# Another order of issue for a fused attention and two-layer-MLP kernel, and a changed rule for sending queued products

## The chip, the cores and the metric

The kernel runs on one core of a Trainium2 chip. The time is the device time of one execution in microseconds (us), the median of several runs. The engines are called by the names that the profile uses: PE (matrix products; PEld its weight loads), DVE, ACT and POOL (the three engines that work element by element), and SP (which issues the transfers). PSUM is the accumulator memory in eight banks, which PE writes and which ACT and DVE read; SBUF is the working memory.

## The reference

A local attention over 7 tokens feeds two MLPs one after the other; all is float32. There are 8192 tokens of 192 values, and both MLPs have a hidden width of 2048.

```python
w = softmax(weight_gen)                       # per token, 8 heads x 7 taps
x1[s] = sum over k of w[s, :, k] * x[s + k - 6]   # 24 values to a head
h = x1 @ moe_w_in;  g = h * sigmoid(h);  x2 = g @ moe_w_out
h = x2 @ moe2_w_in
P = a0 + a1*h + a2*h*h + a3*h*h*h
Q = 1 + abs(b0)*abs(h) + abs(b1)*h*h
out = (P / (Q + 1e-6)) @ moe2_w_out
```

## The kernel before

**Tiling.** The tokens go in 16 batches `b` of 512. In each batch either MLP's hidden width is cut into 8 units `u` of 256, so a unit is a tile of 128 partitions by 1024 values (two PSUM banks, tile `h`). Products are made in two parts (a rounded high part and the rest, the tiles that end in `h` and `l`), so that one matrix product of float32 is several products of PE. PE works as two halves of 64 rows, called lanes; the instructions of a product are dealt to both lanes.

**The operations by letter.** An operation is named letter, unit, batch, as `u3.15`.

| letters | engine | what |
|---|---|---|
| A, K and B, Q | PE | first products of MLP 1 and of MLP 2 into the bank `h`, in two halves |
| S, H, L | ACT, ACT, DVE | MLP 1: silu in place in `h`, its high part `g1h`, its low part `g1l` |
| C, E, I, F and D, P, J, R | PE | second products of MLP 1 and MLP 2 into `acc0`, `acc1` |
| U (line 921), V (line 925) | ACT | MLP 2: `t = a3*h + a2`; `y = abs(b1*h)`. Both read the bank `h` |
| u (line 931), w (line 934) | DVE | `t = t*h`; `t = (t + a1)*h`. Both read the bank `h`; w is the last reader |
| Y, N, G, g | DVE, ACT, ACT, DVE | the denominator, its log, the exponential of minus that, the quotient; all from SBUF |
| h, l | POOL, ACT or DVE; DVE or POOL | high and low part of the quotient (`g2h`, `g2l`) |
| M, m, p, r, a | POOL or DVE | the attention of one token column: two products, three additions |
| T, XH, XL; EC, EM, EA; FC, FT, FE, FA, O | all | turning and splitting the input; handing MLP 1 to MLP 2; turning and storing the output |

**The order of work.** All 3957 operations stand in one written list, `ORDER`. An entry gives the operation, the engine where it may choose (`@1` is the second in its list), and the buffer or bank slot after a colon; `^` loads ACT's tables first and `|` shifts the clocks of PE's lanes. `Plan.run` goes through the list from first to last; each engine gets its own operations in that order and then works through them strictly in turn, waiting at semaphores for what an operation needs. A product entry is not written out at once: `Lanes.add` queues its instructions by lane, and `Lanes.take` writes them as both lanes have something. When an operation of another engine needs a product that is still queued, `Lanes.drain` writes out the queue up to it, even if only one lane has anything:

```python
lanes.drain(past if engine == "PE" else past | need)
```

`Lanes.take` also puts an empty step on SP (line 372) where a bank changes from one pairing of lanes to the other; PE waits for that step.

Of the kernel before, what the change touches and what calls it, by code (L numbers as in the profile page):

```python
# [39 lines left out]
    s0l X.0 q0B0l0:e s1l q0B0l1:d Z.0 q0A0l1:m q0A0l0:q q0O1l1:r q0O0l0:j q0O1l0:g q0O0l1:h q0A1l0:x cl s2l:p  # L40
    q0A1l1:k s0m s0d ^^s0e s0t s0n M0.0@1:v M1.0@1:i cn cz:f q0B0a0 s1m q0B040:B q0B0a1 q0B041 M2.0:b q0A0a0 q0B0h1
    q0A0a1 m2.0@1:l M3.0@1:d m0.0@1:t m1.0@1:y p0.0 p1.0 p2.0 m3.0@1:c r0.0 p3.0 r2.0 a0.0@1:u r3.0@1 r1.0@1 a3.0
    a2.0 a1.0 s1d@1 q0A040:C q0B0h0 q0O0a0 q0B0x1 q0A041 q0O040:D q0B0x0 q0A0h q0O0a1 q0O041 q0A0x W0.0:A T.0 TR.0
    W1.0:B XH0.0:w XL0.0:y A0.0 q0O1a0 ca q0O0h s1e q0O1a1 q0O140:C q0A1a0 X.1 q0O3l0:v s1t q0O141 q0O0x s2m q0O1h@1
    q0O1x cr A1.0:A K0.0 K1.0 A2.0:D K2.0 ^S0.0 S1.0 H0.0:c H1.0:e q1B0l0:i q0O2l0:q q0O3l1:u q0O2l1:h q1O1l0:a
    q1O0l1:s L0.0:t L1.0:j I0.0:C s2d@1 q0A1a1 S2.0 ^^s2e q0A140:A q0A141 q0A1h@1 q0A1x |I1.0 F0.0 A3.0:B C1.0 K3.0
    E0.0 E1.0 C0.0 s2t ^S3.0 H3.0:x q0O2a0 H2.0:c q0O2a1 L3.0:t A5.0:A L2.0:d q0O240:D q0O241 s1n@1 M3.1:m m2.1:g
    M2.1:o m3.1:b p2.1@1 p3.1@1 s2n@1 m1.1:l r2.1@1 M1.1:q p1.1@1 M0.1:l m0.1:h p0.1@1 r0.1@1 r3.1@1 r1.1@1 a0.1:h
    a1.1 a2.1 a3.1 F1.0 K5.0 S5.0 H5.0:k q1B0l1:g s2s q1A0l0:r q1A0l1:b A4.0:B F3.0 F2.0 K4.0 I2.0 L5.0:n q0O3a0
    q0O2h S4.0 q0O3a1 q0O2x H4.0:j q0O340:D q0O341 L4.0:u q1B0a0 q1B0a1 q0O3h@1 q1B040:B q1B041 q0O3x |A6.0:A I3.0  # L50
    K6.0 C5.0 C4.0 C3.0 E5.0 E3.0 E2.0 S6.0 H6.0:p q1A0a0 q1B0h1 q1A0a1 q1B0h0 L6.0:x q1O0l0:v q1O1l1:e X.2 AW.2
    q1A1l0:i q1A1l1:g |||A7.0:D I4.0 K7.0 E4.0 C2.0 E6.0 C6.0 S7.0 H7.0:d q1B0x1 q1A040:A q1B0x0 q1A041 L7.0:o
    ||C7.0 T.1:B ||E7.0 TR.1 F7.0 F6.0 F4.0 I7.0 I6.0 F5.0 I5.0 q1O0a0 q1A0h q1O040:D q1O0a1 q1A0x q1O1a0 XH0.1:q
    q1O041 q1O140:A q1O1a1 q1O0h XL0.1:y q1O141 q1O2l1:r q1O2l0:p q1A1a0 q1O0x q1O1h q1A1a1 EC.0:o q1A140:B q1A141
    q1O1x q1A1h q1A1x ||||||A2.1:D K2.1 EM.0 s3l:d m2.2:t M0.2:w m0.2:v p0.2@1 M1.2:b M2.2:j M3.2:x m3.2@1:u m1.2:e
    p3.2@1 r0.2@1 a0.2:n p1.2@1 r1.2@1 p2.2@1 A1.1:A K1.1 A3.1:B S2.1 H2.1:s L2.1:g q1O2a1 S1.1 q1O2a0 EA.0 s3m
    XH1.0:h A0.1:D K0.1 H1.1:v XL1.0:i K3.1 S0.1 H0.1:u L1.1:a q1O240:A S3.1 H3.1:m q1O3l0:c AW.3 X.3 q1O3l1:o
    L0.1:k B0.0:C Q0.0 q1O241 B5.0:D Q5.0 q1O2h V0.0:l U0.0:t L3.1:p q1O2x Y0.0 F3.1:B I3.1 B3.0:A V5.0:r U5.0:w
    u0.0 w0.0 u5.0 w5.0 r2.2@1 a1.2 r3.2@1 a2.2 s3d@1 a3.2 m0.3:x E3.1 C2.1 Q3.0 F1.1 F2.1 I1.1 B2.0:C C3.1 E2.1
# [218 lines left out]
class Plan:  # L278
# [24 lines left out]

    def run(self, engines, preload, lanes):


        done, final, uses, held = set(), {}, {}, {}
        for entry in ORDER.split():
            name = entry.strip("^|").partition(":")[0].partition("@")[0]
# [4 lines left out]
        for entry in ORDER.split():  # L314
# [3 lines left out]
            if table:  # L318
                preload(table)
# [778 lines left out]
```

## Time and profile before

| | |
|---|---|
| median of 3 runs | 1350.39 us (1350.03 to 1350.97) |
| the profiled execution, its own time | 1347.33 us |
| its span, first to last instruction | 1345.5 us |
| busy: PE, DVE, ACT, POOL | 91%, 83%, 78%, 41% of the span |
| chain that ended last: PE, DVE, ACT, issue | 37%, 28%, 20%, 7% |

The profile is of one execution. Its time is 3.06 us under the median of the runs, and 1.8 us of it lie outside the span. The chain that ended last is followed back from the last instruction, at each step to what released it or to the instruction before it on its engine. A wait names the engine and line whose instruction came last of those waited for.

### The profile page before, as it was taken

The page shows a single profiled execution, that of the slowest core. Times are in us where ns is not written, and L with a number is a line of the kernel's source. Part 1 is how long each engine was busy: PE and PEld are TensorE (multiplying, and loading weights), DVE is VectorE, ACT ScalarE, POOL GpSimd, SP SyncE. Part 2 cuts the span into 40 slices and gives each one's busy share as a digit, 9 for nine tenths or more (in the row PEclk, how much of TensorE's full clock was granted, in tenths as well). Part 3 has the DMA queues.
Part 4 walks back from the last instruction along what each step waited for, and adds up shares of the span by engine and source line. Part 5 has one row for each costly group of instructions (what it writes and reads, how often), then busy time and mean ns, then how long its engine had stood idle before and what let it go on. Part 6 is the DMA issues. An engine that isn't in the chain of part 4 may idle for free.

```text
span 1345.5 us, 24941 instructions
## 1 busy us (share of the span) xinstructions
PE 1219.7 (91%) x10340; PEld 1038.0 (77%) x10340; DVE 1119.9 (83%) x1010; ACT 1047.9 (78%) x1018; POOL 545.7 (41%) x353
## 2 busy tenths in 40 slices
PE   5999998889989999989998898899989999899987
PEld 5668788778867788877786686787768778788866
DVE  7998998887979898887797776967868878887997
ACT  4888897877877886877887776877768778687885
POOL 3973463635454225346236333435312433330142
PEclk9989999999999999999999999999989999999999
DMA  8630011001020100100101010100000101000000
GB/s 224 217 102 1 23 49 41 1 1 50 1 67 1 38 34 1 53 1 20 48 1 50 14 54 1 25 32 2 20 0 2 53 1 50 1 20 1 10 1 36
DMA packets 17752, 45.41 MB, mean 34 GB/s; under 512 B 2412, under 2 KB 9194, under 8 KB 17640
## 3 DMA queue, kind: packets, MB, share of 16 engines
q1 hardware_dynamic: 17640, 43.83, 10.8%
q8 instruction: 81, 1.33, 0.4%
q14 instruction: 31, 0.25, 0.1%
HBM read 31.73 MB, written 7.90 MB: 29 GB/s over the span
## 4 chain that ended last, share of the span: by engine, by line
PE 37%; DVE 28%; ACT 20%; issue 7%; POOL 1%; SPq 0%; POOLq 0%; DVEq 0%; ACTq 0%
PE h L769 19%; PE acc L769 17%; DVE t L931 6%; DVE t L934 5%; ACT y L925 5%; DVE t L951 4%; DVE y L940 4%; ACT t L921 4%; ACT y L945 3%; ACT y L948 2%; DVE g1l L884 2%; DVE g2l L961 2%; ACT g1h L880 2%; ACT h L876 1%; ACT L1061 1%
## 5 line engine op out<-in xcount | busy, mean ns | idle before, releaser
L769 PE MATMUL h<-xh,wa 64*128 64x512 f32 x2048 | 475.0, 401 | 70.2 <-DVE t L934 39.0
L769 PEld LDWEIGHTS h<-xh,wa 64*128 64x128 f32 x2048 | 287.9, 186 | 132.4 <-issue 17.8
L769 PE MATMUL h<-xl,wa 64*128 64x512 f32 x1024 | 317.4, 392 | 0.1
L769 PE MATMUL h<-xh,wb 64*128 64x512 f32 x1024 | 316.4, 391 | 0.0
L769 PE MATMUL acc<-g1h,wo 64*128 64x512 f32 x1536 | 306.8, 397 | 8.1 <-ACT g1h L880 3.6
L769 PE MATMUL acc<-g2h,wo 64*128 64x512 f32 x1536 | 302.4, 397 | 10.0 <-DVE t L934 4.7
L961 POOL TENSOR_TENSOR g2l<-t,g2h 128x1024 fp32r<-128x1024 f32 x65 | 166.9, 2572 | 226.5 <-DVE g2l L961 72.0
L769 PEld LDWEIGHTS acc<-g2h,wo 64*128 64x128 f32 x1536 | 211.6, 186 | 37.8 <-SPq L372 7.9
L931 DVE TENSOR_TENSOR t<-t,h 128x1024 f32<-128x1024 f32 x128 | 155.4, 1215 | 101.0 <-ACT y L925 84.1
L769 PEld LDWEIGHTS acc<-g1h,wo 64*128 64x128 f32 x1536 | 214.5, 187 | 29.0 <-ACT g1h L880 6.3
L769 PE MATMUL acc<-g1l,wo 64*128 64x512 f32 x1024 | 219.1, 401 | 7.4 <-DVE g1l L884 5.8
L711 POOL TENSOR_TENSOR pr<-xw,aw 128x768 f32<-128x768 f32 (+1 forms) x90 | 149.9, 1678 | 181.8 <-PE acc L769 107.2
L769 PE MATMUL acc<-g2l,wo 64*128 64x512 f32 x1024 | 218.5, 396 | 3.8 <-ACT t L921 1.5
L884 DVE TENSOR_TENSOR g1l<-h,g1h 128x1024 fp32r<-128x1024 f32 x128 | 155.0, 1217 | 53.4 <-ACT g1h L880 47.8
L921 ACT ACTIVATE t<-h,a_sb 128x1024 f32<-128x1024 f32 x128 | 153.5, 1201 | 47.4 <-PE h L769 35.0
L925 ACT ACTIVATE y<-h,b_sb 128x1024 f32<-128x1024 f32 x128 | 141.5, 1110 | 60.8 <-DVE t L934 32.5
L940 DVE SCALAR_TENSOR_TENSOR y<-y,b_sb 128x1024 f32<-128x1024 f32 x128 | 179.7, 1410 | 6.2 <-ACT y L925 6.2
L876 ACT ACTIVATE h<-h 128x1024 f32<-128x1024 f32 x128 | 129.3, 1012 | 71.2 <-PE h L769 62.5
L951 DVE SCALAR_TENSOR_TENSOR t<-t,a_sb,y 128x1024 f32<-128x1024 f32 x128 | 181.7, 1431 | 3.5 <-ACT y L948 3.2
L945 ACT ACTIVATE y<-y,c_sb 128x1024 f32<-128x1024 f32 x128 | 145.7, 1148 | 43.1 <-DVE y L940 42.4
L436 POOL TENSOR_SCALAR g2h<-t 128x1024 fp32r<-128x1024 f32 x56 | 72.3, 1294 | 253.3 <-DVE t L951 182.6
L769 PEld LDWEIGHTS h<-xl,wa 64*128 64x128 f32 x1024 | 163.6, 186 | 12.8 <-DVE xl L803 1.0
(79 smaller groups left out, 1985.5 us busy)
## 6 DMA issues: line engine op xcount, KB each, us to landing
xw<-in_x_dram SPq DMA_DIRECT2D x14, 960.0 KB, 5.5
raw<-in_moe_w_out_dram SPq DMA_DIRECT2D x16, 383.5 KB, 6.4
out_dram<-of SPq DMA_DIRECT2D x15, 384.0 KB, 3.0
e<-e SPq DMA_DIRECT2D x32, 128.0 KB, 2.3
raw<-in_moe_w_in_dram SPq DMA_DIRECT2D x16, 255.9 KB, 6.7
raw<-in_moe_w_in_dram SPq DMA_DIRECT2D x4, 511.8 KB, 6.7
aw<-wsm SPq DMA_DIRECT2D x14, 112.0 KB, 2.8
sm<-in_weight_gen_dram SPq DMA_DIRECT2D x3, 448.0 KB, 3.8
```

What stands on the lines that cost most here:

```text
L436: pool.tensor_scalar(out=out, in0=in_, scalar1=1.0, scalar2=0.0, op0=ALU.mult, op1=ALU.add)
L711: e.tensor_tensor(out=p.rearrange("p k (h g) -> p k h g", g=G), in0=st[xw][:, j + k0:j + k0 + n, :].rearrange("p k (h g) -> p k h g", g=G) ...
L769: return pe.matmul(out=out, lhsT=w, rhs=x, start=start, stop=stop)
L876: act.activation(out=st[hb], in_=st[hb], func=AF.Silu)
L884: dve.tensor_tensor(out=t, in0=st[hb], in1=st[gh].bitcast(F32), op=ALU.subtract)
L921: act.activation(out=q, in_=st[hb], func=AF.Identity, scale=a_sb[:, 3:4], bias=a_sb[:, 2:3])
L925: act.activation(out=q, in_=st[hb], func=AF.Abs, scale=b_sb[:, 1:2])
L931: dve.tensor_tensor(out=st[t], in0=st[t], in1=flat(), op=ALU.mult)
L940: dve.scalar_tensor_tensor(out=st[y], in0=st[y], scalar=b_sb[:, 0:1], in1=st[y], op0=ALU.add, op1=ALU.mult)
L945: act.activation(out=st[y], in_=st[y], func=AF.Ln, scale=c_sb[:, 0:1], bias=1.0 + 1e-6)
L951: dve.scalar_tensor_tensor(out=st[t], in0=st[t], scalar=a_sb[:, 0:1], in1=st[y], op0=ALU.add, op1=ALU.mult)
L961: e.tensor_tensor(out=q, in0=st[t], in1=st[gh].bitcast(F32), op=ALU.subtract)
```

## The change

Two things change. First, `ORDER` is another list of the same 3957 operations. Second, `Plan.run` no longer writes out queued products when an operation of another engine needs them: it puts that operation, and all of other engines behind it, into a list `later`, and sends them once the products that they need have been written. A product that needs an operation in `later` sends that list up to it first. The lane clock also counts differently where one lane is empty. The table loads marked by `^` go with their operation.

```diff
+        later = []
+
+        def send():
+            _, after, engine, table, fn = later.pop(0)
+            lanes.drain(after)
+            if table:
+                preload(table)
+            fn(engines[engine])
+
...
-            if table:
-                preload(table)
...
             engine = names[int(e or 0)]
-            lanes.drain(past if engine == "PE" else past | need)
-            if engine == "PE" and name[0] != "W":
-                lanes.add(name, fn(engines[engine]), bars)
+            if engine != "PE":
+                later.append((name, past | need, engine, table, fn))
             else:
-                if engine == "PE":
+                while any(x[0] in need or x[0] in past for x in later):
+                    send()
+                lanes.drain(past)
+                if name[0] == "W":
                     lanes.drain()
-                fn(engines[engine])
+                    fn(engines[engine])
+                else:
+                    lanes.add(name, fn(engines[engine]), bars)
+            while later and not lanes.waiting(later[0][1]):
+                send()
+        while later:
+            send()
         lanes.drain()
...
-        self.clock[r] = max(self.clock[r], self.clock[1 - r] - 1) + turns if not self.queue[1 - r] else self.clock[r] + turns
+        self.now = max(self.now, self.clock[r])
+        self.clock[r] = self.now + turns
+
+    def waiting(self, names):
+        return any(self.left.get(n) for n in names)
...
-        while any(self.left.get(n) for n in (self.left if names is None else names)):
+        while self.waiting(self.left if names is None else names):
             r = int(self.clock[1] < self.clock[0])
-            if not self.queue[r]:
-                self.clock[r] = self.clock[1 - r]
-                r = 1 - r
-            self.take(r)
+            self.take(r if self.queue[r] else 1 - r)
```

All lines of `ORDER` change. A stretch of batch 15 of MLP 2 before and after:

```diff
-    Y0.15 V3.15:s g2.15 Y3.15 g1.15 U3.15:w N0.15 h2.15@1:o G0.15 U6.15:m V6.15:f g0.15 u6.15 Y6.15 B5.15:D P7.14
-    P5.14 P6.14 Q5.15 D4.14 u3.15 w6.15 N3.15 h0.15@1:q N6.15 G3.15 l2.15@1:u h1.15:l w3.15 V5.15:n |D2.15:A P2.15
...
+    B5.15:D P4.14 P7.14 D7.14 D4.14 D5.14 Q5.15 N1.15 V3.15:k G1.15 N0.15 U6.15:l V6.15:y Y3.15 g1.15 l2.15@1:c
+    u6.15 w6.15 G0.15 h1.15@1:s N3.15 g0.15 U3.15:w h0.15@1:v U5.15:g V5.15:t G3.15 Y6.15 N6.15 G6.15 l1.15@1:f
+    u3.15 w3.15 Y5.15 g3.15 l0.15:a g6.15 R2.15:A J2.15 J1.15 J4.14 D1.15 P2.15 D0.15 |B4.15:C P1.15 D2.15 Q4.15
```

Its beginning and its end before and after:

```diff
-    s0l X.0 q0B0l0:e s1l q0B0l1:d Z.0 q0A0l1:m q0A0l0:q q0O1l1:r q0O0l0:j q0O1l0:g q0O0l1:h q0A1l0:x cl s2l:p
...
+    s0l X.0 s1l q0B0l0:u q0B0l1:w Z.0 q0A0l0:g q0A0l1:i s2l:o q0O0l0:h q0O1l1:t q0O0l1:m q0O1l0:v cl q0A1l0:r s0m cn
...
-    D4.14 N7.14 G7.14 FE.14 u7.14 w7.14 g7.14 h7.14@2:b FA.14 l7.14:l ||D7.15 ||J7.15 R7.15 ||P7.15 FC.15:u FT.15:D
-    O.14 O.13 FR.15 FE0.15 FE1.15@1 FA0.15 FA1.15 O0.15 O1.15
...
+    u7.15 w7.15 g7.15 h7.15@2:x l7.15:c ||||P4.15 J4.15 R4.15 |J7.15 FT.14:C ||R7.15 FR.14 D7.15 P7.15 FC.15:f
+    ||FT.15:D FE.14@1 FA.14 O.13 O.14 FR.15 FE0.15 FE1.15 FA0.15 FA1.15 O0.15 O1.15
```

Counted over both texts of `ORDER`:

| | before | after |
|---|---|---|
| M on DVE, of 64 | 18 | 22 |
| m on DVE, of 64 | 20 | 25 |
| p on DVE, of 64 | 24 | 25 |
| r on DVE, of 64 | 20 | 27 |
| a on DVE, of 64 | 26 | 32 |
| h on POOL, ACT, DVE | 56, 50, 22 | 51, 45, 32 |
| l on DVE, POOL | 63, 65 | 62, 66 |
| EC on ACT, DVE | 13, 3 | 11, 5 |
| FC on ACT, DVE | 6, 10 | 11, 5 |
| FE on ACT, DVE | 7, 10 | 9, 8 |
| M, m, p, r, a, h, l on DVE between A0.3 and A0.5 | 23 | 34 |
| loads of ACT's tables | 91 | 85 |
| units in the order V U u w | 36 | 58 |
| units in the order U V u w | 65 | 39 |
| units in the order U u V w | 7 | 10 |
| units in the order U u w V | 20 | 21 |
| entries from U to u, median | 6 | 9 |
| entries from V to u, median | 4 | 7 |

## Rows read from the trace of the kernel before

**Rows 1.** The page, part 1: busy time, share of the span, instructions.

```profile
PE 1219.7 (91%) x10340; PEld 1038.0 (77%) x10340; DVE 1119.9 (83%) x1010; ACT 1047.9 (78%) x1018; POOL 545.7 (41%) x353
```

**Rows 2.** Windows by stage: stretch, length, busy of PE, PEld, DVE, ACT, POOL, clock, DMA.

```profile
29.00:120.00 91.00, 82.86 (x623) 63.32 (x623) 83.19 (x92) 73.86 (x83) 59.55 (x48) 0.94 0.41 130
120.00:760.00 640.00, 588.37 (x5085) 503.81 (x5084) 546.50 (x474) 508.24 (x484) 290.14 (x183) 1.00 0.08 26
760.00:1326.00 566.00, 521.21 (x4418) 447.98 (x4416) 458.76 (x402) 445.61 (x426) 180.62 (x105) 0.98 0.06 16
1326.00:1345.50 19.50, 12.81 (x110) 8.98 (x108) 10.13 (x12) 7.59 (x8) 2.41 (x1) 0.93 0.16 61
```

**Rows 3.** The page, part 4: the chain that ended last, by engine.

```profile
PE 37%; DVE 28%; ACT 20%; issue 7%; POOL 1%; SPq 0%; POOLq 0%; DVEq 0%; ACTq 0%
```

**Rows 4.** Groups by form: busy, mean ns | idle before them, and who ended it.

```profile
L921 ACT ACTIVATE t<-h,a_sb 128x1024 f32<-128x1024 f32 x128 | 153.5, 1201 | 47.4 <-PE h L769 35.0 <-DVE t L951 3.8 <-DVE g2l L961 3.8
L925 ACT ACTIVATE y<-h,b_sb 128x1024 f32<-128x1024 f32 x128 | 141.5, 1110 | 60.8 <-DVE t L934 32.5 <-DVE t L931 11.0 <-PE h L769 10.5
L931 DVE TENSOR_TENSOR t<-t,h 128x1024 f32<-128x1024 f32 x128 | 155.4, 1215 | 101.0 <-ACT y L925 84.1 <-ACT t L921 14.1 <-PE acc L769 2.6
L934 DVE SCALAR_TENSOR_TENSOR t<-t,a_sb,h 128x1024 f32<-128x1024 f32 x128 | 163.5, 1278 | 4.7 <-ACT y L925 1.2
```

**Rows 5.** The chain in order of time, three places: start us, us, what.

```profile
102.48 0.97 ACT y L925
...
103.54 0.06 DVE t L931
...
888.61 1.21 ACT t L921
889.81 1.01 ACT y L925
...
890.90 1.23 DVE t L931
...
892.16 1.29 DVE t L934
...
893.59 1.45 PE h L769 x10
...
1268.33 1.01 ACT y L925
...
1269.37 1.23 DVE t L931
```

**Rows 6.** All waits, two of them: us in total, times, longest us.

```profile
PE h L769 <- DVE t L934: 39.0, 28, 3.8
...
PEld h L769 <- SPq L372: 16.3, 39, 1.9
```

**Rows 7.** Groups by form, the operations that change their engine (columns of Rows 4).

```profile
L711 DVE TENSOR_TENSOR pr<-xw,aw 128x768 f32<-128x768 f32 x18 | 18.4, 1026 | 2.9 <-PE acc L769 1.6 <-DMA xw<-in_x_dram 1.3
L711 DVE TENSOR_TENSOR pr<-xw,aw 128x576 f32<-128x576 f32 x20 | 17.1, 866 | 0.8 <-PE acc L769 0.8
L725 DVE TENSOR_TENSOR pr<-pr 128x384 f32<-128x384 f32 x20 | 14.3, 716 | 0.2 <-POOL pr L721 0.2
L731 DVE TENSOR_TENSOR ao<-pr 128x192 f32<-128x192 f32 x26 | 11.3, 437 | 0.0
L438 DVE CAST g2h<-t 128x1024 fp32r<-128x1024 f32 x22 | 21.2, 969 | 0.2
L438 DVE COPY of<-acc 128x1024 f32<-128x1024 f32 x10 | 12.2, 1218 | 3.4 <-PE acc L769 3.4
L434 ACT ACTIVATE g2h<-t 128x1024 fp32r<-128x1024 f32 x50 | 52.4, 1053 | 8.4 <-DVE t L951 8.3
L434 ACT ACTIVATE of<-acc 128x1024 f32<-128x1024 f32 x6 | 6.1, 1022 | 4.8 <-PE acc L769 4.7
L1061 ACT ACT_TABLE_LOAD x46 | 59.0, 1283 | 1.5 <-PEq L1082 0.7
```

More of the change, by code (lines that the diff above doesn't have):

```diff
@@ L45 @@
[L45 to L59, printed above, removed]
@@ new lines @@
+    N7.10 FE.9 A1.12:C m3.13:r p3.13 FA.9 l2.10:e EM.11 A2.12:D K1.12 D3.10 O.9 X.14 EA.11 G6.10 G5.10 g5.10
+    XH1.11:g h4.10:v XL1.11:r K2.12 J4.10 A0.12:A P2.10 D4.10 ^S1.12 S2.12 H1.12:n g6.10 l3.10:k K0.12 R3.10
+    h6.10@1:a H2.12:c S0.12 H0.12:p r3.13 L1.12:x B2.11:C P3.10 Q2.11 l4.10@1:f L2.12:i r2.13@1 a2.13 a3.13 L0.12:v
+    U2.11:t V2.11:q B3.11:D R4.10 Q3.11 B0.11:A U3.11:h V3.11:l u2.11 w2.11 h5.10:w l6.10@1:k l5.10@1:j D6.10 Q0.11
+    u3.11 w3.11 Y2.11 Y3.11 ^^G7.10 U0.11:b V0.11:s N3.11 N2.11 G3.11 J5.10 J6.10 C2.12:C E2.12 R6.10 R5.10 E1.12
@@ new lines @@
+    L7.13:c H6.13:a I5.13 I7.13 F7.13 B7.12:A V4.12:w U4.12:f Y5.12 L6.13:d ^^N5.12 G5.12 u4.12 Y4.12 w4.12 g5.12
+    C6.13 E6.13 Q7.12 B6.12:B E7.13 C4.13 J0.12:D E4.13 C7.13 Q6.12 F6.13 J3.12 R0.12 R2.12 F4.13 R3.12 N1.12
+    U7.12:c G1.12 u7.12 V7.12:o E5.13 g1.12 h1.12:k w7.12 U6.12:r N4.12 G4.12 V6.12:t l1.12:h Y7.12 P3.12 T.14:A
+    D2.12 I6.13 F5.13 R1.12 TR.14 I4.13 D1.12 P0.12 P2.12 D3.12 D0.12 Y6.12 u6.12 w6.12 N7.12 XH0.14:e EC.13:l G7.12
+    N6.12 h5.12@2:n XL0.14:y EM.13 AW.15 X.15 O.11 A1.14:B g7.12 A0.14:A G6.12 K1.14 J5.12 J2.12 EA.13 g4.12
@@ new lines @@
+    XH1.13:j XL1.13:o h4.12@2:x l5.12:a ^S1.14 H1.14:l A2.14:C D4.12 L1.14:w K2.14 J4.12 B2.13:B R5.12 Q2.13
+    h7.12@1:u S2.14 H2.14:v U2.13:q l7.12:d M1.15@1:b g6.12 h6.12@1:i L2.14:g l6.12@1:m P1.12 P5.12 K0.14 J1.12
+    B0.13:C D5.12 Q0.13 D6.12 u2.13 w2.13 S0.14 H0.14:s V2.13:k L0.14:t A3.14:B V0.13:r U0.13:h J6.12 K3.14 S3.14
+    Y2.13 ^^N2.13 H3.14:i Y0.13 m1.15@1:c l4.12:n u0.13 w0.13 M0.15:a m0.15:p p0.15@1 D7.12 B1.13:A J7.12 R4.12
+    R6.12 Q1.13 L3.14:f p1.15 V1.13:u Y1.13 r0.15@1 U1.13:p G2.13 N1.13 G1.13 N0.13 u1.13 g2.13 w1.13 g1.13
@@ new lines @@
+    m3.15@1:c C1.14:C E2.14 E0.14 C2.14 R7.12 E1.14 B4.13:B P6.12 P4.12 I1.14 Q4.13 F3.14 P7.12 F0.14 F2.14 B3.13:A
+    I2.14 Q3.13 G0.13 U4.13:k FC.12:l a0.15@1:n u4.13 V4.13:x g0.13 E3.14 B5.13:D V3.13:t U3.13:d w4.13 M3.15@1:g
+    m2.15@1:a u3.13 r1.15@1 a1.15@1 w3.13 A4.14:B I3.14 Q5.13 C3.14 K4.14 ^S4.14 H4.14:f h2.13:v l2.13:i Y4.13
+    A7.14:A C0.14 L4.14:r p3.15@1 M2.15:m r3.15@1 K7.14 I4.14 F1.14 A5.14:B C4.14 U5.13:u S7.14 h0.13@1:w u5.13
+    w5.13 K5.14 I0.14 V5.13:b H7.14:c S5.14 H5.14:f A6.14:D E4.14 p2.15 Y3.13 a3.15 r2.15 L7.14:a K6.14 F4.14
@@ new lines @@
+    L5.14:g l0.13:e Y5.13 a2.15@1 h1.13:r l1.13@1:q S6.14 H6.14:s B7.13:A C7.14 FT.12:B E7.14 L6.14:m Q7.13 F7.14
+    FR.12 I7.14 FE.12@1 FA.12 ^^N3.13 G3.13 V7.13:a N4.13 U7.13:p I5.14 F6.14 B6.13:D D1.13:B P2.13 Q6.13 E5.14
+    C6.14 R2.13 J1.13 N5.13 Y7.13 G5.13 G4.13 u7.13 w7.13 g3.13 h3.13@2:i g5.13 g4.13 T.15:A R0.13 I6.14 TR.15 P0.13
+    F5.14 D2.13 D3.13 U6.13:o V6.13:r XH0.15:b E6.14 C5.14 Y6.13 XL0.15:g J2.13 J3.13 R1.13 A0.15:A J0.13 u6.13
+    h4.13@2:t h5.13:y EC.14:f O.12 EM.14 N6.13 G6.13 w6.13 g6.13 K0.15 D4.13 D5.13 A1.15:D N7.13 G7.13 EA.14
@@ new lines @@
+    XH1.14:c l5.13:e XL1.14:n l3.13@1:x J4.13 K1.15 D0.13 B2.14:C P3.13 P5.13 Q2.14 ^S0.15 H0.15:l h6.13@2:i S1.15
+    H1.15:v L0.15:r g7.13 B0.14:A L1.15:m l4.13@1:f U2.14:j h7.13@1:h u2.14 w2.14 J5.13 Q0.14 U0.14:w V0.14:t
+    V2.14:a A3.15:D P1.13 D6.13 K3.15 J6.13 R3.13 A2.15:C R5.13 K2.15 S3.15 H3.15:s S2.15 H2.15:k u0.14 w0.14
+    l7.13:x Y2.14 Y0.14 L3.15:e l6.13@1:u L2.15:y ^^N0.14 P7.13 P4.13 B1.14:A J7.13 Q1.14 C3.15:D R7.13 U1.14:p
+    u1.14 G0.14 V1.14:x g0.14 w1.14 N2.14 I0.15 R4.13 B3.14:C R6.13 F1.15 Q3.14 V3.14:t D7.13 I3.15 B5.14:A P6.13
@@ L348, in __init__ @@
         self.tc, self.sp = tc, sp
-        self.queue, self.clock, self.left, self.side = ([], []), [0, 0], {}, {}
+        self.queue, self.clock, self.now, self.left, self.side = ([], []), [0, 0], 0, {}, {}
         self.after = mybir.DependencyInfo(mybir.DependencyClass.Sync, mybir.DependencyReason.DATA)
```

399 lines of the change are left out of this document (191 added, 208 removed).

## The prediction

> **What bounds the kernel now.** I read the page's busy times first. No engine is full: PE is busy for 91% of the span, DVE for 83%, ACT for 78%, POOL for 41% [rows 1]. Then the windows: between 29 us (the first product) and 1326 us (the last first-product of MLP 2) PE is busy 82.86 + 588.37 + 521.21 = 1192.4 of 1297 us, so it stands still for 104.6 us there; DVE stands for 208 us, and POOL is busy for at most 65% of a stage [rows 2]. So no one engine's work sets the time. The chain of waits confirms it: its span goes to PE for 37%, DVE 28%, ACT 20% [rows 3], in turns. What sets the time is how often PE runs dry because a bank has not come back, and a bank comes back when U, V, u and w of a unit have read it. The reader should see that in the chain near 889 us: U, then V, then u, then w, and only then PE's ten products of the next unit [rows 5]. In the waits, PE stood 39.0 us in 28 places until a w had ended [rows 6].
>
> **What the trace says of two engines at one bank.** u needs U's result and the bank; nothing in the arithmetic makes it need V. Yet near 889 us DVE starts u at 890.90, 1.1 us after U's end (888.61 + 1.21), when V has ended [rows 5]. In all, DVE stood 84.1 us before u until a V ended, and ACT stood 32.5 + 11.0 = 43.5 us before V until a w or a u ended [rows 4]. I paired the k-th instruction of each of the four lines with the k-th such entry of ORDER: in none of the 512 pairs of (U or V) with (u or w) of one unit do the two run at the same time. So reads of one bank by ACT and DVE do exclude each other in this program, and the old list has 65 units in the order U V u w, where a u is due as soon as U ends. Following the chain, it goes straight from a V to a u 32 times (first near 102 us, last near 1268 us) [rows 5].
>
> The Trainium skill (PSUM — Partial Sum Buffer, section "PSUM bank collisions raise a hardware error") says that no two of TensorE, ScalarE and VectorE may touch a bank's quadrant at once, two reads included, and that software must keep them apart. The trace agrees: 0 of 512 pairs overlap. By that rule the order inside a unit can give nothing, since the four reads follow each other in any order; this is the second rival below.
>
> **The change part by part.**
>
> *Reads of a bank.* Removed: 26 of the 65 units in the order U V u w (39 are left); added 22 in V U u w, 3 in U u V w, 1 in U u w V. Four reads in a row take 1.201 + 1.110 + 1.215 + 1.278 = 4.80 us [rows 4] whatever their order, so a swap alone shortens no bank's time. What can shrink is DVE's and ACT's standing still, since other work now stands in between: from V to u there are 7 entries in the middle where there were 4, from U to u 9 where there were 6. I take half of the 84.1 us before u as gone, 42 us, because the distance nearly doubles; of it the share that DVE has in the chain, 28% [rows 3], reaches the end: -11.8 us. Bounds: 0 (the stalls move to the next operation) and -32 x 1.11 = -35.5 us (every V that stands before a u on the chain is covered). ACT's waits before V I leave as they are (27 units had V after u, 31 have).
>
> *Engines.* DVE takes 4 M, 5 m, 7 r, 6 a and 10 h more and 5 FC fewer: 4 x 1.026 + 5 x 0.866 + 7 x 0.716 + 6 x 0.437 + 10 x 0.969 - 5 x 1.218 = 4.1 + 4.3 + 5.0 + 2.6 + 9.7 - 6.1 = +19.6 us [rows 7]. p, l, EC and FE change by +1, -1, +2, -2 and I take them as nothing. Its 208 idle us between 29 and 1326 us [rows 2] cover that, except where DVE is on the chain: 28% of it, +5.5 us; if no cover is left, +19.6; if it falls into idle time, 0. ACT loses 5 h and 6 table loads and gains 5 FC: -5 x 1.053 - 6 x 1.283 + 5 x 1.022 = -5.3 - 7.7 + 5.1 = -7.9 us [rows 7], at 20% of the chain -1.6 us; bounds -7.9 and 0. POOL loses work and bounds nothing at 41% [rows 1]: 0.
>
> *Queued products.* The `later` list leaves each other engine's own order as ORDER has it; what it moves is PE's instructions. A product that stands behind such an operation in ORDER can now be dealt out together with those before it, so that both lanes have something. No row shows what a forced emptying cost. The step on SP that goes with a change of lanes is waited for 16.3 us in 39 places before first products, in PE's weight loads [rows 6], and most of that lies under products still running. Bounds: -16.3 us (all of it comes back) and +16.3 (as many steps again, uncovered). I take -3, nearer to 0 because PE's own idle time is put down to w and not to the step. Behind an operation that waits in `later` everything of ACT, DVE, POOL and SP in the list is sent later in the program too; as each of these queues keeps its order and waits at semaphores, that costs nothing at run time.
>
> *Clock.* The granted clock is 0.94 in 29 to 120 us and 0.98 in 760 to 1326 us [rows 2], which is the lower of its two levels, 1.2 GHz, for a part of the time, and worth 5.5 + 11.3 = 16.8 us of a PE at full clock. I suppose that such stretches come after PE stood still, so that fewer stalls give fewer of them, and take -2, bounds -16.8 and +16.8 (as much again).
>
> *Start and end.* In the prologue SP's loads and the first M, r and a are reordered among themselves, and s2l goes ahead of two loads of MLP 1's weights; the same bytes come in before the first product, so I take 0, with bounds of 3 us either way. In the last 19.5 us [rows 2] both final copies of the output go to ACT one behind the other where one was on DVE, and FE.14 goes to DVE while DVE has to wait for the last products anyway: 0, bounds 0 and +1.
>
> **Sum.** -11.8 + 5.5 - 1.6 - 3 - 2 = -12.9 us. On the profiled execution: 1347.3 - 12.9 = 1334.4 us. That execution is 3.06 us under the median of the runs, 1350.39; on the median it is 1337.5. I forecast 1336, between them.
>
> **The rivals.**
>
> *DVE becomes what is late (slower).* Place: between A0.3 and A0.5, where M, m, p, r, a, h and l on DVE go from 23 entries to 34; from 120 to 760 us DVE is busy 85% already, from 29 to 120 us 91% [rows 2]. For: 19.6 us more work, and each r or a waits in DVE's queue behind Y, g and w, which free banks and feed PE. Against: 546.5 of 640 us leaves 93 idle [rows 2]. If all of it arrives, 1350.4 + 19.6 = 1370; with half, 1360. It decides once the idle time before u that comes back is less than the added work, that is under 19.6 of the 84.1 us.
>
> *The exclusion can't be ordered away (no change).* Four reads take 4.80 us in any order; DVE's standing before u turns into ACT's standing before U or V, or into DVE's before w. For: V U u w only lets the chain go V, U, u in place of U, V, u. Against: 84.1 us at 41 places is idle time that other DVE work could fill. Then -1.6 + 5.5 - 3 remain, about 0 net: 1351, and 1347 to 1356.
>
> *PE's stalls fall much more.* If the delays that come from this exclusion caused a third of PE's 104.6 idle us and those went, -35 us: 1315; with the clock's 5 us back too, 1310. For: PE's largest wait is for w [rows 6], which sits behind each such delay. Against: w is as often late because DVE is occupied by something else.
>
> **Chances.** The forecast, 1320 to 1347: 0.50. PE's stalls fall much more, 1300 to 1320: 0.16. No change, 1347 to 1356: 0.14. DVE late, 1356 to 1370: 0.20. What a measurement can tell from no change is 0.2%, 2.7 us: faster is under 1347.7, slower over 1353.1. Faster: 0.50 + 0.16 + 0.01 = 0.67; same: 0.09; slower: 0.20 + 0.04 = 0.24. The range leaves out a third of the fast case and a half of the slow one, 0.05 + 0.10: 1306 to 1362; the likeliest case's own range is 1320 to 1347.
>
> **What would show it.** Right: DVE's idle time before u until V falls from 84.1 to about 42 us; DVE's busy time rises by about 20 us to 1140, ACT's falls by about 8 to 1040; PE's idle time from the first product to the last first-product falls by about 13 us; the chain goes from V to u about 20 times and not 32. Wrong in the first step: the idle time before u falls and reappears before w, L or g, with PE as idle as before. Wrong in the second: DVE above 85% with PE's wait for w over 39 us. The forecast fails altogether if the new list moves something that I priced at nothing, a unit's h or l on POOL above all, onto the way to PE: then g2h or g2l stand among PE's longest waits.

## The result and the profile after

The changed kernel takes 1260.31 us (median of 4 runs, 1256.25 to 1265.15) where the kernel before took 1350.21 beside it: a ratio of 0.9335 (0.9299 to 0.9371), 89.9 us less. The forecast was 1336, and the range ended at 1306: the direction was right, the size more than six times too small. The profiled execution took 1258.52 us, 1256.7 of them its span.

The page of the changed kernel, its busy times, answers to [rows 1]; the chain that ended last, to [rows 3].

```profile
PE 1193.0 (95%) x10340; PEld 1020.4 (81%) x10340; DVE 1143.7 (91%) x1037; ACT 1041.0 (83%) x1012; POOL 509.4 (41%) x326
...
PE 62%; DVE 19%; ACT 10%; issue 5%; SPq 2%; POOL 1%; DMA 1%; DVEq 0%; ACTq 0%; POOLq 0%
```

PE has gone from one of three engines that set the time in turns to the one that sets most of it. Its windows, cut where the last first-product of MLP 2 now stands (1236 us, not 1326), answer to [rows 2]:

```profile
29.00:120.00 91.00, 83.44 (x637) 62.93 (x636) 80.94 (x90) 71.22 (x83) 63.42 (x49) 0.95 0.44 136
120.00:760.00 640.00, 619.36 (x5413) 526.85 (x5411) 590.06 (x524) 548.49 (x522) 271.03 (x165) 1.00 0.09 29
760.00:1236.00 476.00, 462.97 (x4084) 407.86 (x4084) 439.44 (x382) 402.57 (x385) 155.15 (x90) 1.00 0.05 15
1236.00:1256.70 20.70, 14.44 (x118) 10.45 (x114) 11.55 (x13) 8.40 (x10) 4.12 (x2) 0.92 0.15 57
```

From 29 us to the last first-product PE is busy 83.44 + 619.36 + 462.97 = 1165.8 of 1207 us. It stands still for 41.2 us, where it was 104.6: 63.4 us of the 89.9 are stalls that went. Another 26.6 us are busy time (1192.4 down to 1165.8).

Why the stalls went shows in the groups by form (columns of [rows 4], whose lines U 921, V 925, u 931 and w 934 are now 938, 942, 948 and 951; the last three rows answer to [rows 7]):

```profile
L938 ACT ACTIVATE t<-h,a_sb 128x1024 f32<-128x1024 f32 x128 | 153.8, 1203 | 24.9 <-PE h L786 15.8 <-DVE pr L738 2.7 <-DVE t L968 2.4
L942 ACT ACTIVATE y<-h,b_sb 128x1024 f32<-128x1024 f32 x128 | 142.2, 1112 | 33.0 <-PE h L786 11.3 <-DVE t L951 11.1 <-DVE t L948 5.0
L948 DVE TENSOR_TENSOR t<-t,h 128x1024 f32<-128x1024 f32 x128 | 155.5, 1215 | 23.5 <-ACT t L938 13.4 <-ACT y L942 8.4 <-issue 0.8
L951 DVE SCALAR_TENSOR_TENSOR t<-t,a_sb,h 128x1024 f32<-128x1024 f32 x128 | 163.6, 1279 | 4.8 <-ACT y L942 1.2
...
L455 DVE CAST g2h<-t 128x1024 fp32r<-128x1024 f32 x32 | 27.8, 870 | 0.4
L742 DVE TENSOR_TENSOR pr<-pr 128x384 f32<-128x384 f32 x27 | 19.4, 728 | 0.4 <-POOL pr L738 0.3
L1078 ACT ACT_TABLE_LOAD x43 | 55.2, 1283 | 1.5 <-PEq L1099 0.7
```

The four reads of a bank take as long as before (1.203, 1.112, 1.215, 1.279 us). With instructions and entries of `ORDER` paired as in the prediction, 6.42 us pass on average from the start of a unit's first read to the end of its last, where 6.63 did, and again none of the 512 pairs overlaps: the bank is read for hardly less long. What changed is what ends the idle time in front of them: DVE waits 8.4 us before u until a V has ended, where it was 84.1; ACT waits 11.1 + 5.0 = 16.1 us before V until a w or a u has ended, where it was 43.5. Of 127.6 us of waits of one engine for the other's read, 24.5 are left. PE's longest wait went with them. The waits of the changed kernel, to be read beside [rows 6]:

```profile
PEld h L786 <- SPq L388: 17.2, 43, 1.1
...
PE h L786 <- DVE t L951: 9.1, 8, 1.7
```

PE stood 39.0 us in 28 places for a w, and now 9.1 us in 8; the step on SP is as it was. Followed back through the whole span, the chain goes straight from a V to a u 2 times, where it was 32. One of the two, in the chain of the changed kernel:

```profile
637.52 1.01 ACT y L942
...
638.56 1.22 DVE t L948
```

### The profile page after: what moved, and what is told of

The parts are those of the page before. It is cut to its first block, busy times and chain, and to the rows that moved or that the text cites. A ratio compares the mean times of both kernels' runs of the same rounds, so it can differ in the third digit from the quotient of the medians.

```text
span 1256.7 us, 24901 instructions
## 1 busy us (share of the span) xinstructions
PE 1193.0 (95%) x10340; PEld 1020.4 (81%) x10340; DVE 1143.7 (91%) x1037; ACT 1041.0 (83%) x1012; POOL 509.4 (41%) x326
## 4 chain that ended last, share of the span: by engine, by line
PE 62%; DVE 19%; ACT 10%; issue 5%; SPq 2%; POOL 1%; DMA 1%; DVEq 0%; ACTq 0%; POOLq 0%
PE acc L786 31%; PE h L786 29%; DVE y L957 3%; DVE t L968 3%; DVE t L948 3%; DVE t L951 2%; DVE g1l L901 2%; ACT y L942 2%; ACT t L938 1%; DVE pr L728 1%; ACT y L962 1%; ACT h L893 1%; ACT g1h L897 1%; ACT y L965 1%; DVE dec L602 1%
## 5 line engine op out<-in xcount | busy, mean ns | idle before, releaser
L786 PE MATMUL h<-xh,wa 64*128 64x512 f32 x2048 | 464.6, 397 | 23.1 <-DVE t L951 9.1
L786 PEld LDWEIGHTS h<-xh,wa 64*128 64x128 f32 x2048 | 284.2, 185 | 76.5 <-SPq L388 17.2
L786 PE MATMUL h<-xh,wb 64*128 64x512 f32 x1024 | 311.5, 389 | 0.0
L786 PE MATMUL acc<-g1h,wo 64*128 64x512 f32 x1536 | 299.0, 393 | 0.5 <-DVE t L951 0.4
L786 PE MATMUL acc<-g2h,wo 64*128 64x512 f32 x1536 | 292.6, 392 | 3.7 <-SPq L388 3.2
L786 PEld LDWEIGHTS acc<-g1h,wo 64*128 64x128 f32 x1536 | 208.9, 185 | 24.5 <-SPq L388 3.8
L786 PE MATMUL acc<-g2l,wo 64*128 64x512 f32 x1024 | 213.7, 393 | 6.0 <-DVE g2l L978 4.1
L786 PE MATMUL acc<-g1l,wo 64*128 64x512 f32 x1024 | 212.4, 397 | 3.1 <-DVE g1l L901 2.6
L728 POOL TENSOR_TENSOR pr<-xw,aw 128x768 f32<-128x768 f32 (+1 forms) x81 | 126.6, 1572 | 138.4 <-DVE t L968 41.4
L948 DVE TENSOR_TENSOR t<-t,h 128x1024 f32<-128x1024 f32 x128 | 155.5, 1215 | 23.5 <-ACT t L938 13.4
L786 PEld LDWEIGHTS h<-xh,wb 64*128 64x128 f32 x1024 | 163.7, 185 | 12.6
L942 ACT ACTIVATE y<-h,b_sb 128x1024 f32<-128x1024 f32 x128 | 142.2, 1112 | 33.0 <-PE h L786 11.3
L951 DVE SCALAR_TENSOR_TENSOR t<-t,a_sb,h 128x1024 f32<-128x1024 f32 x128 | 163.6, 1279 | 4.8 <-ACT y L942 1.2
```

The costliest lines, as they stand in the source:

```text
L728: e.tensor_tensor(out=p.rearrange("p k (h g) -> p k h g", g=G), in0=st[xw][:, j + k0:j + k0 + n, :].rearrange("p k (h g) -> p k h g", g=G) ...
L786: return pe.matmul(out=out, lhsT=w, rhs=x, start=start, stop=stop)
L942: act.activation(out=q, in_=st[hb], func=AF.Abs, scale=b_sb[:, 1:2])
L948: dve.tensor_tensor(out=st[t], in0=st[t], in1=flat(), op=ALU.mult)
L951: dve.scalar_tensor_tensor(out=st[t], in0=st[t], scalar=a_sb[:, 1:2], in1=flat(), op0=ALU.add, op1=ALU.mult)
```

## The experiments

The first theory was the prediction's third rival: the old list's order lets a V on ACT hold up a u on DVE (and a w a V), and all that stands behind the held operation is late with it; the new list spaces them. The rivals were that the gain comes from the other half of the change (`later`, the lane clock), from the split of work among engines, or from better places for other operations. Ratios are to the kernel before on the same chip, with 95% intervals.

**Each half alone.** The new `ORDER` with the old `Plan.run` and lane clock; then the old `ORDER` with the new ones. The edit is either half of the diff above.

> The new list of operations in the old kernel, whose queue of products is still emptied when another engine needs one of them. If the gain of 90 us comes from where the list puts the reads of a bank, nearly all of it is here: 1258 to 1285 us, with DVE's idle time before u until a V ended near the 8 us of the changed kernel. If it comes from the products that are no longer written out early, little is here: 1325 to 1355 us. If each part needs the other, it lies between, and PE's busy time from the first product to the last first-product is longer than in the changed kernel.

> The old list of operations in the new kernel, whose queue of products is not emptied early. If the gain comes from where the list puts the reads of a bank: 1335 to 1355 us, with DVE's idle time before u until a V ended still near 84 us. If it comes from the products that are no longer written out early: 1260 to 1290 us.

The new list alone: 1267.54 us, 0.939 (0.9367 to 0.9414), 81 us less. Its u, by form:

```profile
L931 DVE TENSOR_TENSOR t<-t,h 128x1024 f32<-128x1024 f32 x128 | 155.4, 1214 | 23.7 <-ACT t L921 12.8 <-ACT y L925 8.9 <-issue 0.8
```

The new sending alone: 1367.61 us, 1.0142 (1.0118 to 1.0166), 19 us more and above its range, and u waits as long as ever:

```profile
L948 DVE TENSOR_TENSOR t<-t,h 128x1024 f32<-128x1024 f32 x128 | 155.4, 1215 | 106.4 <-ACT y L942 89.5 <-ACT t L938 15.6 <-PE acc L786 1.2
```

So 81 of the 90 us, and the vanished waits, belong to the list. The list also brings another split of work among the engines, and that split was not run by itself.

**The exclusion taken away.** If reads that exclude each other are the cause, the old list must gain as much when V doesn't read the bank at all. V reads a weight tile in SBUF that never changes, in all units:

```diff
-            act.activation(out=q, in_=st[hb], func=AF.Abs, scale=b_sb[:, 1:2])
+            act.activation(out=q, in_=WA[1][0][:, 0:W2].bitcast(F32), func=AF.Abs, scale=b_sb[:, 1:2])
...
-        plan.op(f"V{u}", b, "ACT", mag, rd=[*ht, *ab], wr=yt)
+        plan.op(f"V{u}", b, "ACT", mag, rd=[("W", 1, "A", 0), *ab], wr=yt)
```

> The old kernel, with V reading 1024 columns of a constant tile of weights in SBUF in place of the bank, so that the denominator is that of other values and no read of V keeps u or w waiting. If the delays that the exclusion puts on u and w are what the old list lost, most of the 90 us come back: 1265 to 1300 us. If the loss is in how products are written out or elsewhere: 1325 to 1350 us.

1253.52 us, 0.9291 (0.9272 to 0.931): 95 us less and below both ranges, with the old list, the old sending and the old engines. By form, no V is left among the largest waits of u, and no reader of a bank among those of V:

```profile
L931 DVE TENSOR_TENSOR t<-t,h 128x1024 f32<-128x1024 f32 x128 | 155.1, 1213 | 27.3 <-ACT t L921 27.1
...
L925 ACT ACTIVATE y<-wa,b_sb 128x1024 f32<-128x1024 f32 x128 | 145.3, 1142 | 3.3 <-PE acc L769 2.3 <-PE tp L782 0.4 <-DVE g2l L961 0.4
```

95 us for 127.6 us of waits [rows 4] is 0.75 us a microsecond. That it is the bank which keeps the two apart shows in the pairs: V runs at the same time as u or w of its unit in 82 of 256 pairs here, and in none when it reads the bank. But the edit does two things more, so not all of the 95 need be the waits: it frees V from waiting for PE's products (10.5 us [rows 4]), and a bank is now read for 5.19 us on average from first read to last (U, u and w alone) where it was 6.63. The new list gains its 81 us without that shorter reading (6.42). The same edit in the changed kernel shows how much each list still has to lose:

> The changed kernel with V reading a constant tile of weights in place of the bank in all units (other values in the denominators). Left of the waits are 8.4 us before u and 11.1 + 5.0 us before V. At 0.75 of 24.5 us: 1238 to 1247 us. If the new list has already hidden what can be hidden and PE's own work is now the limit (41 us idle from the first product to the last first-product): 1250 to 1260 us.

1255.01 us, 0.9309 (0.9276 to 0.9342), 5 us under the changed kernel by the medians, 4 by the ratios, whose intervals overlap, so that the 5 us are not clear of noise. Without the shared read the two lists are alike (1253.5 and 1255.0). With it, the old one pays 95 us and the new one about 5. That is the core of the case. One reserve: PE is busy for 1194.1 of 1251.3 us in the one and 1188.9 of 1247.7 in the other, 95%, so both stand near PE's own work, and that may be a part of their being alike. The two runs that follow stand further from it (PE idle for 80 and 103 us, where it is 57 and 59 here).

**The two kinds of wait apart.** The same edit in only the 65 units with the order U V u w, and in only the 27 units where V stands after u.

```diff
+            src = WA[1][0][:, 0:W2].bitcast(F32) if (b, u) in OFF else st[hb]
-            act.activation(out=q, in_=st[hb], func=AF.Abs, scale=b_sb[:, 1:2])
+            act.activation(out=q, in_=src, func=AF.Abs, scale=b_sb[:, 1:2])
...
```

`OFF` is the set of these units; their V is also declared to read the weight tile and not the bank.

> The old kernel with V reading a constant tile of weights in place of the bank, but only in the 65 units that have U V u w (so the values of their denominators are others). It takes away the 84.1 us that DVE stood before u until a V ended, and leaves the 43.5 us that ACT stood before V. If a microsecond that a queue stands there arrives at the end nearly whole, at the 0.75 that all V off the bank gave (95 of 127.6 us): 1280 to 1298 us. If only the share of the chain that DVE has arrives, 28%, as the prediction had it: 1318 to 1330 us.

> The same, only in the 27 units whose V stands behind u (in these the values of the denominators are others). It takes away the 43.5 us that ACT stood before V until a u or w ended, and leaves the 84.1 us before u. At 0.75: 1308 to 1325 us. At ACT's share of the chain, 20%: 1336 to 1346 us. If this and the run with 65 units add up to the 95 us of all V off the bank, the two delays are independent.

The 65 units: 1288.61 us, 0.9564 (0.9535 to 0.9593), 61 us less; DVE's idle time before u falls from 101.0 to 30.1:

```profile
L933 DVE TENSOR_TENSOR t<-t,h 128x1024 f32<-128x1024 f32 x128 | 155.3, 1215 | 30.1 <-ACT t L922 29.9
```

The 27 units, in 20 of which V and not w is the bank's last reader: 1319.81 us, 0.9794 (0.9767 to 0.9822), 30 us less; in the other 101 no wait for a u or a w is among the three largest before V:

```profile
L927 ACT ACTIVATE y<-h,b_sb 128x1024 f32<-128x1024 f32 x101 | 111.5, 1108 | 15.1 <-PE h L770 12.0 <-PE acc L770 1.9 <-DVE pr L722 1.1
```

61 and 30 add to 91, nearly the 95 of all units: two costs beside each other. One is worth 61 / 84.1 = 0.73 of DVE's waits for V (0.86 of the 70.9 us of idle time that went), the other 30 / 43.5 = 0.69 of ACT's.

**Filling the wait without removing it.** In the old list, 19 operations of DVE that were ready stand ahead of a u that waits:

```diff
-    U1.5:l h7.4:a V1.5:u u1.5 Y0.5 N0.5 w1.5
+    U1.5:l h7.4:a V1.5:u Y0.5 u1.5 N0.5 w1.5
```

> The old kernel, with one operation of DVE moved ahead of u in 19 of the 65 units: the next Y, g, p, r or u of another unit in DVE's own order that the trace shows ready by then. Nothing else is moved, and the exclusion stays. It can fill some 20 us of the 101 us that DVE stood before u. If standing still counts nearly whole, 1328 to 1338 us; at 28%, 1341 to 1346 us; if the stall only moves to the next operation, 1347 to 1352 us.

1346.07 us, 0.9977 (0.996 to 0.9994), 3.8 us less, with 101.0 - 86.5 = 14.5 us less idle time before u:

```profile
L705 DVE TENSOR_TENSOR t<-t,h 128x1024 f32<-128x1024 f32 x128 | 155.5, 1216 | 86.5 <-ACT y L699 68.8 <-ACT t L695 14.8 <-PE acc L543 2.6
```

That is 0.26 us a microsecond, close to the 28% that the prediction used; the interval allows from 0.06 to 0.37. It is the worth of these 19 moves and not of filling as such, for the new list takes no read away either and only puts other work into the wait. One difference shows in the traces: after the 19 moves u starts as late as before, on average 1.77 us after the end of its U (1.76 in the kernel before); in the changed kernel it is 1.38. That this is what makes the moves cheap was not tested.

**Swapping U and V.** In the 65 units of the old list, U and V exchange places, each with its slot:

```diff
-    U1.5:l h7.4:a V1.5:u u1.5
+    V1.5:u h7.4:a U1.5:l u1.5
```

> The old kernel, with U and V exchanged in the list in the 65 units that had U V u w, so that they have V U u w. If the four reads of a bank only follow each other in any order, this alone gives nothing: 1342 to 1358 us, and DVE's idle time before u is put down to U in place of V. If the order inside a unit matters by itself, the 32 places where the chain goes from V to u are saved at 1.1 us each: 1310 to 1330 us.

1368.79 us, 1.0146 (1.0122 to 1.0169), 20 us more and above both ranges. By form:

```profile
L699 ACT ACTIVATE y<-h,b_sb 128x1024 f32<-128x1024 f32 x128 | 142.2, 1112 | 105.4 <-DVE t L708 34.8 <-PE h L543 30.1 <-PE acc L543 22.2
...
L705 DVE TENSOR_TENSOR t<-t,h 128x1024 f32<-128x1024 f32 x128 | 155.4, 1215 | 122.8 <-ACT t L695 114.4 <-PE acc L543 4.6 <-issue 3.5
```

The wait of u only changes its name, from V to U (114.4 us). And V, issued earlier, now waits 22.2 us for a second product: what stood in its SBUF slot was still being read. Another order inside the unit gains nothing here, but the loss is mixed with the slots', since a slot belongs to a place in the list. A swap with the slots left in place wasn't tried.

**The place of u in the new list.** In 97 units of the changed kernel u, and w if it is near, move directly behind the later of U and V, some 9 entries earlier on average. That is closer than in the old list: from V to u the median is 1 entry, where the old list has 4 and the new one 7.

```diff
-    U0.5:f V0.5:x Y2.5 m1.8@1:u g7.4 Y0.5 R4.4 N2.5 h7.4@1:a U1.5:l G2.5 N0.5 G0.5 R5.4 C2.6 J7.4 u0.5 w0.5
+    U0.5:f V0.5:x u0.5 w0.5 Y2.5 m1.8@1:u g7.4 Y0.5 R4.4 N2.5 h7.4@1:a U1.5:l G2.5 N0.5 G0.5 R5.4 C2.6 J7.4
```

> The changed kernel with u, and w with it where it stood within three entries, moved in the list to directly behind the later of U and V in the 97 units where u stands behind both; on average 8.9 entries earlier. It undoes the longer distance from U and V to u, which the prediction took as the gain, and the rest of the new list stays. If that distance is what the new list gives, DVE's idle time before u comes back towards 84 us or more and the time goes towards 1290 to 1320 us. If standing still before u counts little and the gain is in the rest of the list, 1258 to 1275 us.

1480.75 us, 1.0993 (1.0958 to 1.1028): 220 us more than the changed kernel, far above the old list and above both ranges. Its u by form, then its busy times, then its mean granted clock:

```profile
L722 DVE TENSOR_TENSOR t<-t,h 128x1024 f32<-128x1024 f32 x128 | 155.9, 1219 | 191.8 <-ACT t L712 130.8 <-ACT y L716 54.7 <-PE acc L560 5.1
```

```profile
PE 1263.2 (86%) x10340; PEld 1048.9 (71%) x10340; DVE 1139.7 (77%) x1037; ACT 1042.7 (71%) x1012; POOL 502.8 (34%) x326
```

```profile
core 0: 1476.3 us, clock 0.938
```

Idle time before u rises by 191.8 - 23.5 = 168.3 us, most of it now a wait for U and not for V. PE stands still for 1476.3 - 1263.2 = 213.1 us, 149.4 more than in the changed kernel, and is busy for the same products 70.2 us longer, about what the ratio of the granted clocks gives (0.938 for 0.993); the two make the 220. u itself is not late: it starts on average 0.89 us after the end of its U, sooner than in the changed kernel (1.38). Late is what stands behind it in DVE's queue while DVE waits. PE now stands longest for the low part of MLP 1's `g1`, which DVE makes: 30.8 + 26.1 us, where it was 4.8 + 2.6. So the new list depends on u standing back. How much of its gain the step from the old distance to the new one is, this run does not measure, since it goes past the old distance.

**More work for DVE.** Each addition `a` on DVE is done three times, in either kernel:

```diff
-                e.tensor_tensor(out=st[ao][:, j], in0=p[:, 0], in1=p[:, 1], op=ALU.add)
+                for _ in range(3 if e is dve else 1):
+                    e.tensor_tensor(out=st[ao][:, j], in0=p[:, 0], in1=p[:, 1], op=ALU.add)
```

> The old kernel with each of the 26 additions a on DVE done three times: 52 x 0.437 = 22.7 us more work on DVE, all from SBUF, in the attention, whose result is due late. If added work of DVE counts by its share of the chain, 28%: 1352 to 1359 us. If it counts nearly whole, as standing still does: 1365 to 1374 us. If DVE's idle time covers it: 1347 to 1352 us.

> The same in the changed kernel: 32 additions a on DVE three times each, 64 x 0.437 = 28.0 us more work on DVE, which is busy 91% there. By its share of the chain, 19%: 1263 to 1268 us. Nearly whole: 1280 to 1290 us. Covered by idle time: 1257 to 1263 us.

In the kernel before: 1362.79 us, 1.0108 (1.0073 to 1.0143), 12.4 us more, between its ranges. Its `a` by form, 36.7 us where it was 11.3 [rows 7]:

```profile
L732 DVE TENSOR_TENSOR ao<-pr 128x192 f32<-128x192 f32 x78 | 36.7, 471 | 1.8
```

In the changed kernel: 1283.88 us, 0.9515 (0.9487 to 0.9544), 23.6 us more than without it:

```profile
L749 DVE TENSOR_TENSOR ao<-pr 128x192 f32<-128x192 f32 x96 | 44.7, 469 | 3.1 <-PE acc L787 0.6
```

25.4 us of work cost 12.4 (0.49) with the old list; 44.7 less the 13.0 that they take in the changed kernel is 31.7 us, and costs 23.6 (0.74) with the new. By the intervals of the ratios the rates are 0.39 to 0.76 and some 0.57 to 0.96: that the new list has less room in DVE is likely, and not shown.

**The lane clock and `later`, one by one.** The new list with the new clock alone and with `later` alone; the old list likewise. The clock is this edit, and `later` is the rest of the diff of `Plan.run`:

```diff
-        self.clock[r] = max(self.clock[r], self.clock[1 - r] - 1) + turns if not self.queue[1 - r] else self.clock[r] + turns
+        self.now = max(self.now, self.clock[r])
+        self.clock[r] = self.now + turns
...
-            if not self.queue[r]:
-                self.clock[r] = self.clock[1 - r]
-                r = 1 - r
-            self.take(r)
+            self.take(r if self.queue[r] else 1 - r)
```

> The new list in the old way of writing out products (queue emptied early), with the new formula for the lane clock alone. If the clock is what the second part gives, 1257 to 1264 us; if it is the products no longer written out early, 1264 to 1272 us.

> The changed kernel with the list of waiting operations, but with the old formula for the clock of a lane when the other is empty. If what the second part of the change gives (1267.5 to 1260.3 us) comes from the products no longer being written out early, this is as fast as the changed kernel, 1256 to 1264 us; if it comes from the clock, 1264 to 1270 us.

> The old list, products written out early as before, with the new formula for the lane clock alone. The old list with both new rules ran 18.9 us slower. If the clock is what costs there: 1362 to 1372 us. If it is the list of waiting operations: 1345 to 1353 us.

> The old list with the list of waiting operations, products no longer written out early, but with the old formula for the lane clock. If the waiting operations are what cost with the old list: 1362 to 1372 us. If it is the clock: 1345 to 1353 us. Both between, some 1357 us each, if each costs half.

| list | old sending, old clock | new clock alone | `later` alone | both |
|---|---|---|---|---|
| old | 1348.4 to 1350.4 | 1350.1 | 1399.71 | 1367.61 |
| new | 1267.54 | 1260.98 | 1266.98 | 1260.31 |

With the new list the clock gives 6.6 us without `later` and 6.7 with it, and `later` gives nothing; the intervals of the ratios overlap, but both pairs agree. In the busy times of the new list, first with the old clock and then with the new, the clock shows as PE's own work done in 8.0 us less, and the other engines alike:

```profile
PE 1204.2 (95%) x10340; PEld 1039.9 (82%) x10340; DVE 1145.2 (90%) x1037; ACT 1041.0 (82%) x1012; POOL 510.7 (40%) x326
```

```profile
PE 1196.2 (95%) x10340; PEld 1025.6 (81%) x10340; DVE 1145.6 (91%) x1037; ACT 1041.1 (83%) x1012; POOL 512.1 (41%) x326
```

With the old list the clock gives nothing (1.0013, 0.9994 to 1.0032), but `later` costs 51 us (1.0389, 1.036 to 1.0417), far more than was expected, of which the new clock takes 32 back. The waits for the step on SP grow with it. First the one of the kernel before that [rows 6] lacks, then `later` with both new parts, then `later` with the old clock:

```profile
PEld acc L769 <- SPq L372: 15.8, 37, 1.0
```

```profile
PEld h L786 <- SPq L388: 28.4, 82, 1.9
...
PEld acc L786 <- SPq L388: 25.8, 66, 2.3
```

```profile
PEld acc L788 <- SPq L388: 46.8, 113, 2.3
...
PEld h L788 <- SPq L388: 46.4, 117, 1.6
```

32.1 us in 76 places become 54.2 in 148 and 93.2 in 230: 22.1 us more for 19 us, 61.1 us more for 51. The changes of pairing are no more frequent: the traces have 691 such steps on SP in each kernel with the old list and 680 in those with the new. It is the waits for them that grow. The changed kernel has 17.2 + 15.4 = 32.6 us. And the longer time stands in PE's busy time, not in its idle time. The busy times of `later` with both new parts, then with the old clock, beside [rows 1]:

```profile
PE 1238.0 (91%) x10340; PEld 1012.0 (74%) x10340; DVE 1118.3 (82%) x1010; ACT 1049.4 (77%) x1018; POOL 543.7 (40%) x353
```

```profile
PE 1273.2 (91%) x10340; PEld 1015.0 (72%) x10340; DVE 1116.3 (80%) x1010; ACT 1050.4 (75%) x1018; POOL 537.5 (38%) x353
```

The same products take 1219.7, then 1238.0, then 1273.2 us, while PE is idle for 125.8, 128.4 and 127.9 us of the spans. One lane that works while the other waits would look like this, but the waits were not changed alone: that they are the cause is argued from how the two grow together, and products dealt out less evenly to the lanes are a rival. Why the new list's products don't get more such waits wasn't tried.

## Why the prediction was wrong in size

**The mechanism was right.** The prediction read that ACT and DVE exclude each other at a bank, that DVE stood 84.1 us before u for a V, and that the new list spaces them. All of that held, and taking the shared read away bears it out.

**The step that failed is the term *Reads of a bank*, -11.8 us: both of its factors, and its bound.**
- *How much of the wait goes.* Half of 84.1 us was taken, because the distance nearly doubles; 90% went (8.4 us left). The waits of ACT before V, "as they are", fell from 43.5 to 16.1, although the number of units with V after u hardly changed. Together 103 us went where 42 were forecast.
- *What a microsecond of it is worth.* DVE's 28% share of the chain was used as the rate. V off the bank gave 0.75 for all units, 0.73 and 0.69 for the two kinds; only the 19 moves into the wait gave about 28% (0.26). u and w stand at the head of DVE's queue while they wait, and everything behind them is late too. 103 x 0.75 = 77 us, near the 81 us of the list alone; the sum is not closed, since DVE's added work (below) would come off the 77.
- *The bound.* -35.5 us counted a V's length at each of the 32 direct steps from V to u on the chain. The chain shows the one wait that decided at a moment, not the delays that earlier waits had already put into the queues. V off the bank gave 95 us, nearly three times the bound, and the list alone 81.

**Engines.** The work was right: DVE +23.8 us (forecast +19.6), ACT -6.9 (forecast -7.9). The rate was not: 28% was taken for DVE, 0.49 was measured in the old list and 0.74 in the new. By these, an estimate, DVE's added work cost 12 to 18 us, not 5.5, and the list gains in spite of it. No run gave the old split of engines to the new list, so this cost was not measured by itself.

**Queued products.** -3 us was forecast; some -6.6 came, from the lane clock and not from `later`. The upper bound, "as many steps again, uncovered", +16.3, is what the sending does to the old list, +19 with both parts and +51 with `later` alone, and the time stands in PE's busy time. The steps themselves stayed 691.

**Clock.** -2 us was forecast. The granted clock went from 0.94, 1.00 and 0.98 in the three stages to 0.95, 1.00 and 1.00. The lower level took 5.5 + 11.3 = 16.8 us' worth before; now it is 83.4 and 463 us of busy PE at 0.95 and 1.00, or about 4. So about 12 us of the gain are PE's clock, which came with the stalls that went; PE's stalls were not changed without the rest. They are a part of the 26.6 us of busy time.

**Start and end.** The last stage has 20.7 us for 19.5, 1.2 us longer, just over its bound of +1. The first product into a bank `h` starts at 28.98 us, where it was 27.34: 1.6 us later, within the bound of 3.

**The rivals.** "PE's stalls fall much more" was the right one, and itself too small: it let a third of 104.6 us go, and 63.4 went. "The exclusion can't be ordered away" fell. The Trainium skill (PSUM — Partial Sum Buffer, section "PSUM bank collisions raise a hardware error") has the rule behind it, and the trace before agreed with it (0 of 512 pairs overlap); the four reads indeed still take 4.81 us, and swapping U with V only makes u wait for U, as that rival said. But that a bank's reads can't overlap doesn't mean that an engine must stand while it waits for its turn: about 5 us of 95 are left. "DVE becomes what is late" didn't come, since 75.7 of the 84.1 us before u went and it needed fewer than 19.6 to go.

**What stays open.** How the new list makes even the 24.5 us of waits that are left cheap: about 5 us, 0.2 us a microsecond, against 0.75 in the old; PE's own work, 95% of the span, may hide the rest. How the gain is divided among u's place, V's, the work in between and the other split among the engines wasn't taken apart.

## What to carry to other kernels

When an operation at the head of an in-order queue waits for another engine, don't price that wait at the engine's share of the chain, here 28%. A microsecond of it was worth 0.26 when 19 single operations were moved into it, 0.75 when its cause was taken away, and 1.3 (220 us for 168.3) when u was moved ahead: no one rate carries over. Price it by taking the cause away on the chip (here one operation reads from somewhere else), and do it in the old and the new kernel: alike times there and unlike times before say what an order of issue is worth, as long as no other limit holds both. Rules for sending and a list made with them belong together; here `later` cost the old list 51 us and the new one nothing.

## What the runs showed of the hardware

- Taking one of four reads of a PSUM bank (ACT and DVE, each about 1.2 us, never two at once) away gave 95 of 1349 us with the old list, and about 5, not clear of noise, with the new one.
- With 168.3 us more idle time of DVE before u came 220 us more time: PE stood 149.4 us longer, and its busy time for the same products grew by 70.2 us at a granted clock of 0.938 for 0.993.
- A wait for a bank's change from one pairing of lanes to the other took some 0.4 us on average (93.2 us in 230 places). 61.1 us more of such waits came with 51 us more time, at the same 691 changes, and with PE busy 53.5 us longer for the same products.
